# Windowed attention cut into 32-query by 64-key blocks ahead of a tuned Mish feed-forward

## The chip, the cores and the metric

The kernel runs on one core of one Trainium2 chip. The metric is the device time of one execution in microseconds (us). Three executions of the kernel before took 891.72, 894.63 and 894.75 us; the median is 894.63 us.

## The reference, cut to what matters

```python
# q, k, v: (8 batches, 8 heads, 576 positions, 64 per head)
scores = q @ k.transpose(0, 1, 3, 2) / np.sqrt(64)
rel = pos[:, None] - pos[None, :]
mask_plain = (rel >= 0) & (rel < 32)                        # heads 0 to 3
mask_dil = (rel >= 0) & (rel < 128) & (rel % 4 == 0)        # heads 4 to 7
scores = np.where(mask, scores, -1e9)
attn = np.exp(scores - scores.max(-1)); attn /= attn.sum(-1) + 1e-9
x = (attn @ v) laid out as (4608 tokens, 512)
h = x @ w_in                                                # w_in: 512 x 2048
g = h * np.tanh(softplus(h))
out = g @ w_out                                             # w_out: 2048 x 512
```

A query of a plain head sees itself and the 31 keys behind it. A query of a dilated head sees 32 keys too, every fourth one. If the positions are sorted by their residue modulo 4, the dilated heads have the same narrow band within each residue. The weights arrive as 8-byte numbers.

## The kernel before, in words

The 4608 tokens are worked off as 16 units of 288 tokens, two (half 0 and half 1) for each batch. For each unit the attention of eight heads (four pairs of heads: two plain, two dilated) gives x in a transposed layout, split in two float16 parts (hi and lo). The feed-forward then runs on TensorE (PE): `ff1` (L938) multiplies x by w_in, 192 matmuls of 128x128 weights and 288 columns for a unit, ScalarE (ACT) applies Mish, `gate` or `gate_of` splits the result in two float16 parts, and the second product follows. For units 0 to 7 that is `ff2` (L1126): 192 matmuls of 288 columns. For units 8 to 15 (the constant `SEVENS`) it is `product` (L1077): seven half-size products in place of eight, 336 matmuls of 144 columns, with sums of g made by `gate_sums` (L1057) on VectorE (DVE) and sums of w_out made once by `w_sums` (L991, L995) after `rescale` (L976).

The attention works on blocks of 96 queries by 128 keys (plain) and 72 queries by up to 104 keys (dilated, one block for each residue), one pair of heads at a time:

- `scores_of_pair` (L687): the two heads of a pair lie in the upper and the lower 64 partitions, so each matmul uses 64 rows of the array. In units 0 to 2 ("direct") q and k are float32. In the other 13 units ("converted") `prep` scales q and k and splits them in float16 parts (ACT L571, L600, L603, L609; DVE L612, L615; the scale comes by `tops_of`, PE L361 and L368), and each block takes three float16 matmuls.
- `scores` (DVE L711, L717, L719), `exps` (ACT), `transpose_p` (PE L807 for direct units; ACT L795, DVE L797 and a DMA for the others).
- `values` (L830 direct, L836 converted): probabilities times v, 65 columns (64 and the sum), one block and head after another on the full array. For converted units that is three float16 matmuls for each.
- `transpose_x` (DVE L851 writes its input; L869, L891 to L895), which fills x.

The weights (16 halves) are loaded, joined from two words and split by `w_load`, `w_max`, `w_scale`, `w_words` (POOL L446, DVE L448 and L450) and `w_split` (ACT L457, DVE L459) in the first part of the run. `keep_warm` (L1157) issues matmuls of zeros while PE would have nothing else.

The order of all work is a written table, `ORDER`: each word is one step of one function ("ff0.6" is the next step of `ff1(0, 6)`), and each engine executes its instructions in the order in which the table issues them.

Of the kernel before, what the change touches and what calls it, by code (L numbers as in the profile page):

```python
# [10 lines left out]
F16 = mybir.dt.float16  # L11
# [26 lines left out]
MASKED = -2.0 ** 30  # L38
# [3 lines left out]
ld0 mf cs0 cs1 xa1 xa0 kw32 kw22 sp0.1=0 cs3 lv0 lv1 sc0.1 lv0 sp0.0=1 lv1 wl0.3.1 ex0.1 sc0.0 ex0.1 sp0.2=2 ww0.3.1  # L42
sc0.2 wl0.3.0 pr1 ex0.0 pr0 ex0.2 wl0.0.0 ld1 pr0 sp0.3=3 tp0.1=0 ww0.3.0 sc0.3 ex0.2 pr0=2 pr0 ex0.0 tp0.1 tp0.2=1
ex0.3 tp0.2 pr1 pr1 pr0 wl0.0.1 wm0.3.1 va0.2=0 pr0 ex0.3 va0.2 va0.1=1 tp0.3=2 wm0.3.0 va0.2 kw8 tx0.2=3 tp0.0=0
va0.1 va0.1 tx0.1=1 ww0.3.0 wl0.1.1 tp0.3 va0.3=2 ww0.3.1 tx0.2 tx0.2 tp0.0 va0.0=0 tx0.1 ww0.3.0 va0.3 tx0.1 va0.3
kw15 sp1.0=2 wm0.3.0 ww0.3.0 ww0.3.0 va0.0 va0.0 kw5 sp1.2=0 tx0.2 sp1.1=3 wm0.0.0 tx0.1 ww0.0.1 ws0.3=1 ww0.0.0 ld2
sc1.0 ex1.0 tp1.0=2 wm0.0.1 ww0.3.0 sc1.2 tx0.3=0 ex1.2 sc1.1 kw20 pr1=3 tp1.0 kw3 tx0.0=2 tx0.3 tx0.0 ws0.3 ex1.1
sp1.3=1 lv2 tx0.0 tx0.0 pr1 sc1.3 tp1.2=3 ww0.3.1 tp1.2 kw23 va1.2=2 ex1.3 va1.0=3 ww0.0.0 kw15 tp1.3=1 va1.2 va1.0
wp0.3.0 ww0.0.1 tp1.3 va1.2 tx0.3 tx0.3 kw8 ws0.0=2 kw3 tx1.2=1 kw4 tp1.1=0 wp0.3.1 ww0.0.1 ws0.0 wl0.1.0 va1.0
wp0.3.1 tx1.2 kw24 tx1.2 ww0.0.0 tx1.0=2 wp0.3.0 tp1.1 wl0.2.0 va1.3=3 wm0.1.0 va1.1=0 tx1.0 va1.3 va1.1 tx1.0 va1.3  # L50
ww0.1.0 wl0.2.1 wm0.1.1 kw29 ff0.6=3 tx1.0 va1.1 tx1.2 tx1.1=0 tx1.3=2 ww0.1.0 ww0.1.1 ww0.1.1 wp0.0.1 wp0.0.1 ww0.2.0
ff0.6 tx1.3 tx1.1 tx1.1 tx1.3 ws0.1=1 ws0.1 wl1.3.1 wp0.0.0 tx1.3 kw4 ff1.7=0 ff1.7 wm0.2.0 wp0.0.0 ww0.2.1 ww0.2.0
wm0.2.1 ww0.2.1 ff0.1=1 ws0.2=2 ws0.2 ff0.1 wl1.3.0 ft lv2 fs0.0 ff1.1=2 ff1.1 ww0.2.0 fs1 ff1.7 ff1.0=0 pr2 fs0.1
ff1.0 wp0.2.0 ww0.1.1 wp0.2.0 ww0.2.1 fs0.2 ff1.1 ww1.3.1 ff1.6=2 fs0.3 wl1.2.0 wp0.1.1 ff1.0 ff0.6 ww1.2.0 gt1.0=0
ff0.1 fs0.4 wp0.1.1 pr2 ww0.1.0 ff1.6 sp2.3=0 wp0.1.0 ff0.7=3 ww1.3.0 ff0.7 sc2.3 ff0.0=1 wp0.2.1 wp0.1.0 ff1.6 ff0.0
wp0.2.1 wl1.2.1 wm1.3.0 gt1.0 ww1.3.0 ff0.7 wm1.3.1 ww1.3.1 ff1.5=2 ff1.4=3 gt1.3=1 ex2.3 wm1.2.0 ff1.4 gt1.3 ws1.3=0
ff1.5 ff0.0 ww1.3.0 ff1.2=1 ff1.2 gt0.0=2 wm1.2.1 ws1.3 ff1.4 ff1.5 wp1.3.0 gt0.3=3 ww1.2.1 tp2.3=0 ww1.2.0 ww1.3.1
ww1.2.0 wp1.3.0 wp1.3.1 ff1.3=3 tp2.3 ff1.3 ww1.2.1 wl1.0.0 sp2.0=2 pr2 ff1.3 wp1.3.1 ws1.2=0 ff0.5=3 ff0.5 sc2.0
ff1.2 lv3 ww1.2.1 ws1.2 wm1.0.0 ww1.0.0 cs2 ex2.0 wl1.0.1 ff0.2=1 gt0.0 wp1.2.1 gt0.3 ff0.3=0 tp2.0=2 ff0.2 ff0.3
wp1.2.0 ww1.0.1 ww1.0.0 ff0.5 sp2.2=3 tp2.0 pr2=2 ff0.2 wm1.0.1 wp1.2.0 wl1.1.1 wp1.2.1 ff0.4=1 ff0.3 pr2 wl1.1.0 xa3  # L60
va2.0=2 ww1.1.1 gt1.1=4 va2.3=0 va2.0 ww1.0.1 va2.3 gt0.1=5 ww1.0.1 ff0.4 va2.0 sc2.2 va2.3 sp2.1=2 wm1.1.1 wm1.1.0
ff0.4 gt0.2=6 fo0.2.0=1 gt0.1 fo0.3.0 ws1.0=0 gt0.2 ww1.1.0 ex2.2 sc2.1 ws1.0 fo0.3.1 ld3 ex2.1 fo0.3.2 wp1.0.1
# [36 lines left out]
va7.1 pr8 tp7.0=1 ff6.0 fo5.1.3 tp7.0 ff6.1=1 ld9 ff6.1 fo5.3.2 fo5.0.3 sp8.0=2 tx7.1=0 sc8.0 ff6.0 tp7.0=1 ff6.4=0
# [95 lines left out]
QB = 96  # L195
# [1021 lines left out]
```

## Time and profile before

| | before |
|---|---|
| median of three runs | 894.63 us |
| profiled execution, span from first to last instruction | 892.4 us |
| PE busy | 873.6 us (98%) |
| PE weight loads busy | 737.9 us (83%) |
| DVE busy | 705.7 us (79%) |
| ACT busy | 621.1 us (70%) |
| POOL busy | 74.2 us (8%) |

The profile's times are those of one execution, which is given by its span alone; the median stands 2.2 us above that span. Busy PE counts a matmul from its start to its modelled end, so a column of means is longer than the distance between two matmuls that follow each other; the chain of waits gives the distance. PE stands in nearly all of the chain, so the places to look at are the distances on PE, and the early stretch, where the chain's end alone does not say what set the pace.

### The profile page before, as it was taken

The numbers are of one execution on the slowest core, as the hardware profiler recorded it, in microseconds if no ns is written. First come the engines' busy times: TensorE is split into PE (matmuls) and PEld (weight loads), VectorE is DVE, ScalarE is ACT, GpSimd is POOL, SyncE is SP. The second block draws the span as 40 slices with busy tenths as digits, with TensorE's granted clock in tenths as the row PEclk, the third lists the DMA queues.
The fourth block names the chain that finished last, engine by engine and source line by source line (L and its number), as shares of the span: only waits on it lengthen the run. The fifth ranks groups of instructions, "written<-read, shape, count | busy, mean of one in ns | idle before, by whom it ended". The sixth has DMA issues, their size and how long they took to land. (4 is left out here: it accounts for less than half of the span.)

```text
span 892.4 us, 23856 instructions
## 1 busy us (share of the span) xinstructions
PE 873.6 (98%) x10335; PEld 737.9 (83%) x10338; DVE 705.7 (79%) x1035; ACT 621.1 (70%) x924; POOL 74.2 (8%) x123
## 2 busy tenths in 40 slices
PE   9898989999999999999999999999999999999997
PEld 8776768888788878888888788998899898988897
DVE  4888976778879678878899889997999888855453
ACT  5867765874676667797876876858877886844342
POOL 3237463000000000000000000000000000000000
PEclk9999999999999999999999999999999999999999
DMA  9652540326432635253632325235523522122001
GB/s 312 238 189 95 146 143 10 105 72 137 104 68 52 128 74 140 50 130 60 157 85 52 87 43 148 60 86 116 102 67 70 126 58 58 32 59 64 2 15 41
DMA packets 154049, 84.36 MB, mean 95 GB/s; under 512 B 117496, under 2 KB 149848, under 8 KB 153944
## 3 DMA queue, kind: packets, MB, share of 16 engines
q1 hardware_dynamic: 153944, 82.83, 37.5%
q8 instruction: 81, 1.33, 0.6%
q14 instruction: 24, 0.20, 0.1%
HBM read 49.02 MB, written 9.44 MB: 66 GB/s over the span
## 5 line engine op out<-in xcount | busy, mean ns | idle before, releaser
L938 PE MATMUL b<-x,w 128*128 128x288 f16 x3072 | 392.1, 287 | 0.0
L938 PEld LDWEIGHTS <-w 128*128 128x128 f16 x3072 | 298.0, 98 | 75.1 <-issue 0.2
L1126 PE MATMUL b<-g,w 128*128 128x288 f16 x1536 | 198.9, 287 | 0.0
L1126 PEld LDWEIGHTS <-w 128*128 128x128 f16 x1536 | 148.5, 98 | 37.7 <-issue 0.2
L944 ACT ACTIVATE hm<-b,fs 128x576 f32<-128x576 f32 x128 | 92.5, 738 | 78.1 <-PE b L938 63.3
L1077 PE MATMUL b<-g,w 128*128 128x144 f16 x1536 | 101.8, 226 | 0.4 <-DVE y L1096 0.3
L1077 PEld LDWEIGHTS <-w 128*128 128x128 f16 x1536 | 97.6, 98 | 1.6 <-issue 0.6
L1051 DVE SCALAR_TENSOR_TENSOR g<-hm,sg,g 128x1152 f16<-128x1152 f32 (+1 forms) x64 | 79.5, 1261 | 23.3 <-ACT g L1049 23.2
L1049 ACT ACTIVATE g<-hm,sg 128x1152 f16<-128x1152 f32 (+1 forms) x64 | 71.4, 1129 | 15.2 <-PE b L1077 12.0
L758 ACT ACTIVATE sb<-sb,ln_p 72x832 f32<-72x832 f32 (+3 forms) x52 | 46.1, 893 | 18.5 <-DVE sb L719 18.3
L1028 DVE SCALAR_TENSOR_TENSOR g<-hm,sg,g 128x1152 f16<-128x1152 f32 x32 | 46.5, 1462 | 7.1 <-ACT g L1026 7.1
L797 DVE TENSOR_TENSOR p<-sb,p 96x768 f16<-96x768 f32 (+3 forms) x52 | 46.7, 903 | 5.9 <-ACT p L795 5.8
L719 DVE TENSOR_TENSOR sb<-sb,nm 96x512 f32<-96x512 f32 (+4 forms) x64 | 49.2, 768 | 2.2
L717 DVE TENSOR_REDUCE nm<-sb 96x4 f32<-96x512 f32 (+4 forms) x64 | 48.8, 763 | 1.8
L1091 ACT ACTIVATE y<-b,fo 128x288 f32<-128x288 f32 x32 | 25.1, 783 | 35.8 <-PE b L1077 35.7
L1057 DVE TENSOR_TENSOR hm<-hm 128x576 f32<-128x576 f32 x64 | 47.5, 753 | 0.8
L869 DVE TENSOR_TENSOR x<-xs,x 96x384 f16<-96x384 f32 (+1 forms) x52 | 32.0, 615 | 15.9 <-ACT x L867 15.8
L851 DVE TENSOR_TENSOR xs<-b,rec 72x512 f32<-72x512 f32 (+1 forms) x64 | 39.7, 621 | 5.8
L867 ACT CAST x<-xs 96x384 f16<-96x384 f32 (+1 forms) x52 | 29.0, 558 | 21.7 <-DMA x<-x 9.4
L621 POOL MEMSET vh<- 128x12 f16 x26 | 4.2, 167 | 452.9 <-ACT vh L571 390.8
L1077 PE MATMUL b<-g,g 128*128 128x144 f16 x576 | 40.3, 226 | 1.1 <-ACT y L1091 1.1
L795 ACT CAST p<-sb 72x832 f16<-72x832 f32 (+3 forms) x52 | 40.8, 791 | 0.5 <-DMA pT<-p 0.2
(177 smaller groups left out, 1198.1 us busy)
## 6 DMA issues: line engine op xcount, KB each, us to landing
qn<-in_qT SPq DMA_DIRECT2D x16, 576.0 KB
raw<-in_w_out SPq DMA_DIRECT2D x16, 512.0 KB
raw<-in_w_in SPq DMA_DIRECT2D x12, 512.0 KB
out_T<-y SPq DMA_DIRECT2D x32, 144.0 KB
out_T<-y SPq DMA_DIRECT2D x16, 288.0 KB
knd<-in_kdT SPq DMA_DIRECT2D x16, 208.0 KB
vdn<-in_vd SPq DMA_DIRECT2D x7, 416.0 KB
vn<-in_v SPq DMA_DIRECT2D x7, 384.0 KB
```

Of the source, the lines that this page charges most:

```text
L717: nc.vector.tensor_reduce(nm[:nq, :, j:j + n], x, axis=AX.X, op=ALU.max, negate=True)
L719: nc.vector.tensor_tensor(blocked(sb, c0, n, w), x, nm[:nq, :, j:j + n].unsqueeze(3).broadcast_to([nq, 2, n, w]), op=ALU.add)
L758: nc.scalar.activation(x, x, AF.Exp, bias=ln_p[:nq])
L797: nc.vector.tensor_tensor(lo, src, hi, op=ALU.subtract)
L938: nc.tensor.matmul(ph[:, h, :HT], w1[j][:, c, wi, k * P:(k + 1) * P], x_of(d, xi, c), start=(n == 0), stop=(n == len(seq) - 1))
L944: nc.scalar.activation(d["m"][p][:, half, k0:k0 + 2], ph[:, :, :HT], AF.Mish, scale=d["fs"][:, j:j + 1])
L1028: nc.vector.scalar_tensor_tensor(g[:, 1], m, sg, g[:, 0], ALU.mult, ALU.subtract)
L1049: nc.scalar.activation(hi, src, AF.Identity, scale=sg)
L1051: nc.vector.scalar_tensor_tensor(lo, src, sg, hi, ALU.mult, ALU.subtract)
L1057: nc.vector.tensor_tensor(a, a, b, op=op)
L1077: nc.tensor.matmul(acc[e], left(l, e, p, wi)[:, k * P:(k + 1) * P], right(gi, k), start=(n in opens and p == 0 and q == 0), stop=(last and ...
L1126: nc.tensor.matmul(po[:, :HT], w2[:, e, j, wi, k * P:(k + 1) * P], d["g"][j][:, gi, k, :], start=(j == 0 and n == 0), stop=(j == NCH - 1 a ...
```

## The change

It does five things.

1. The attention of a unit is cut anew. A block is 32 queries by 64 keys; three blocks stand side by side as 96 queries. Plain and dilated heads become two *kinds*, and one step handles all four heads of a kind instead of one pair. A matmul of the scores (L573) has 64 rows, 32 columns of weights and 64 streamed columns (56 for the dilated kind of half-0 units from unit 3); the head picks the row half and the block picks one of three 32-column strips of the array. `values` (L673) does the same: 64 keys as rows, 32 queries as weights, 65 streamed columns, so a block's six matmuls lie on six different tiles of the array.
2. Scores are float32 in all units. The scaling and splitting of q and k, and `tops_of`, are gone; the scale of v alone comes by a bf16 matmul (L325). `spread_q` copies the plain q by residue on POOL (L476).
3. v is loaded as 64-key windows, 16 (half 0) or 21 (half 1) of them, that overlap: 12 or 16 DMAs for a unit in runs of 256 bytes. The split of v works on 2048 or 2688 elements of a partition.
4. `SEVENS` begins at unit 3 instead of 8, so `rescale` and all of `w_sums` now come ahead of unit 3's products.
5. `ORDER` is a new table. Biased exponentials, subtraction on PE and the float16 subtraction on PE (L739, L752, L891) are gone.

```diff
-    SEVENS = range(8,16)
+    SEVENS = range(3, 16)

+    def spread_q(u):
+        qp = d["qp"] = pool.tile([P, 2 * HT], F32, name="qp")
+        nc.gpsimd.tensor_copy(qp.rearrange("p (b r i) -> p b r i", r=NR, i=SQ // NR),
+                              d["q"][:, :2 * HT].rearrange("p (b i r) -> p b r i", r=NR, i=SQ // NR))

     def loads_v(u):
+        for h in range(2):
+            for a in range(2):
...
+                nc.sync.dma_start(o[:, :n0], bass.AP(row.tensor, row.offset, [[w, WK], [SQ * w, n0], [1, D]]))
+                for s in range(ns):
...
+                    nc.sync.dma_start(o[:, n0:].rearrange("k (r s) d -> k r s d", s=ns)[:, :, s],
+                                      bass.AP(row.tensor, row.offset, [[w, WK], [2 * RB * w, NR], [1, D]]))

     def prep(u):
-        mr = yield from tops_of(m, 6)
...
+        o = yield from over_partitions(m, 2)
...
-        for x, hi, lo in qparts:
-            nc.vector.tensor_tensor(lo, x, hi, op=ALU.subtract)
...
-        for c, x in zip(ksl, kn):
-            nc.vector.scalar_tensor_tensor(kl[:, c], x, s[:, 1:2], kh[:, c], ALU.mult, ALU.subtract)

-    def scores_of_pair(u, pair):
...
-                for i, (qi, ki) in enumerate([(1, 0), (0, 0), (0, 1)]):
-                    products.append((o, d["q2"][hs, qi, pair, q0:q0 + nq], d["k2"][hs, ki, k0:k0 + nk], i == 0, i == 2))
+    def scores_of_kind(u, kind):
...
+        for a in range(2):
+            for t in range(nb):
+                for s in range(NS):
...
+                    for h in range(2):
+                        hs = slice(h * D, (h + 1) * D)
+                        c = (a * nb + t) * WK
+                        q = d["q"] if kind else d["qp"]
+                        nc.tensor.matmul(pt[s * SQ:(s + 1) * SQ, h, c:c + w], q[hs, q0:q0 + SQ], d["k"][kind][hs, k0:k0 + w],
+                                         start=not d["direct"], stop=True, skip_group_check=True)

     def scores(u, kind):
+            nc.vector.scalar_tensor_tensor(o, i, 1.0 / math.sqrt(D), m, ALU.mult, ALU.add)
+        nc.vector.tensor_reduce(nm[:, :, :n], src, axis=AX.X, op=ALU.max, negate=True)
+        nc.vector.tensor_tensor(dst, src, nm[:, :, :n].unsqueeze(3).broadcast_to([QB, 2, n, w]), op=ALU.add)

     def values(u, pair):
-                for i, (p, vi) in enumerate([(0, 1), (0, 0), (1, 0)]):
-                    c = ((p * 2 + h) * nb + g) * rows
-                    nc.tensor.matmul(avv[:, h, j], pp[:nk, c:c + P], vv[vi][:nk, j, hh, :], start=(i == 0), stop=(i == 2))
+        passes = [(None, 0)] if d["direct"] else [(0, 1), (0, 0), (1, 0)]
+        for t in range(nb):
+            for i, (pi, vi) in enumerate(passes):
+                for s in range(NS):
+                    for h in range(2):
...
+                        nc.tensor.matmul(avv[s * SQ:(s + 1) * SQ, h, t], p[:hk.stop - hk.start],
+                                         vv[vi][hk, window(d, kind, t, s), a, :],
+                                         start=(i == 0), stop=(i == len(passes) - 1), skip_group_check=True)

 ORDER = """
-ld0 mf cs0 cs1 xa1 xa0 kw32 kw22 sp0.1=0 cs3 lv0 lv1 sc0.1 lv0 sp0.0=1 lv1 wl0.3.1 ex0.1 sc0.0 ex0.1 sp0.2=2 ww0.3.1
+wl0.0.1 wm0.0.1 mf ld0 ww0.0.1 qp0 ld0 mf cs1 kw43 sp0.0=0 cs0 wl0.0.0 ld0 ld0 ww0.0.0 ww0.0.1 wm0.0.0 ww0.0.1 ld1
...
```

How the order moves is seen at three places. On the queue of the loads (SP) at the start of the program, the kernel before asks for q, k and v of the first two units (qn, knp, knd; w2 is v's home here) and then for weights:

```order
L487 DMA qn_113<-in_qT 128x1152
L489 DMA knp_115<-in_kT 128x2x288
L492 DMA knd_117<-in_kdT 128x4x72 x2
L513 DMA w2_92<-in_v 128x256
L513 DMA w2_92<-in_v 128x2x256
L514 DMA w2_92<-in_vd 72x4x256
L513 DMA w2_92<-in_v 128x3x256
L514 DMA w2_92<-in_vd 104x4x256
L383 DMA raw_229<-in_w_in 128x512 x2
```

The changed kernel, from the same place, alternates weights with q and k of two units:

```order
L343 DMA raw_111<-in_w_in 128x512 x2
L461 DMA qn_140<-in_qT 128x1152
L466 DMA knp_146<-in_kT 128x2x288
L343 DMA raw_267<-in_w_in 128x512 x2
L470 DMA knd_141<-in_kdT 128x4x80 x2
L461 DMA qk_276<-in_qT 128x1152
L466 DMA knp_285<-in_kT 128x2x320
L343 DMA raw_346<-in_w_in 128x512 x2
L470 DMA qk_276<-in_kdT 128x4x112 x2
L494 DMA w2_90<-in_v 64x8x64
L497 DMA w2_90<-in_vd 64x4x64 x2
```

The first half of w_in moved from behind v to the head of the queue, and v of the first unit moved behind three halves of the weights.

On DVE, also at the start, the kernel before begins with maxima of scores (nm from the banks b); the first instruction on a weight is L448, twenty rows on:

```order
L717 TENSOR_REDUCE nm_214<-b0_70 96x2x2
L717 TENSOR_REDUCE nm_214<-b0_70 96x2
L717 TENSOR_REDUCE nm_236<-b1_71 96x2x2
L717 TENSOR_REDUCE nm_236<-b1_71 96x2
L717 TENSOR_REDUCE nm_252<-b2_72 72x8
```

In the changed kernel the weights' L408 and L410 (L448 and L450 before) stand first, and the subtraction of the maxima (L599) is DVE's in the first units too:

```order
L408 SCALAR_TENSOR_TENSOR w10_86<-w10_86,raw_111 128x1024
L410 SCALAR_TENSOR_TENSOR raw_111<-raw_111,w10_86 128x1024
L598 TENSOR_REDUCE nm_281<-b0_70 96x2x6
L599 TENSOR_TENSOR sb_280<-b0_70,nm_281 96x2x6x64
L408 SCALAR_TENSOR_TENSOR w10_86<-w10_86,raw_267 128x1024
```

The work on the weights moved ahead of the first scores.

On PE, in the middle of a late unit, a dilated pair's scores of the kernel before (24 matmuls, each with its load of weights q2) follow the small matmul of `tops_of` and stand among half-size products:

```order
L1077 MATMUL b2_72<-g1_100,w2_92 128x144
L368 MATMUL b1_71<-cd_10660,ones_74 128x6
L687 LDWEIGHTS q2_10037
L687 MATMUL b3_73<-k2_10087,q2_10037 72x72
L687 LDWEIGHTS q2_10037
L687 MATMUL b3_73<-k2_10087,q2_10037 72x72
```

In the changed kernel the 48 float32 scores of a kind are one row (each brings its own weights):

```order
L773 LDWEIGHTS w10_86
L773 MATMUL b0_70<-x_8583,w10_86 128x288
L573 MATMUL b2_72<-knd_9115,qn_9114 32x56 x48
L912 LDWEIGHTS w2_90
L912 MATMUL b3_73<-g1_98,w2_90 128x144
```

A little ahead of it the values of one dilated pair begin (72 such pairs of rows follow one another there):

```order
L773 LDWEIGHTS w10_86
L773 MATMUL b1_71<-x_8583,w10_86 128x288
L673 LDWEIGHTS pT1_2309
L673 MATMUL b0_70<-vh_8839,pT1_2309 32x65
L673 LDWEIGHTS pT1_2309
```

The four stretches of scores of a unit became two, and the matmul of `tops_of` is gone. Of a whole program, PE's rows hold 1,344 float32 score matmuls (two passes each in the trace) and 3,276 float16 value matmuls now, where there were 1,092 float16 score and 1,092 value matmuls for the converted units.

## Rows read from the trace of the kernel before

**Rows 1.** The page: span, engines, chain by engine and by line.
```profile
span 892.4 us, 23856 instructions
PE 873.6 (98%) x10335; PEld 737.9 (83%) x10338; DVE 705.7 (79%) x1035; ACT 621.1 (70%) x924; POOL 74.2 (8%) x123
PE 43%; ACT 0%; DVE 0%; issue 0%; DVEq 0%
```
**Rows 2.** The chain in order of time, late units: start us, us, what.
```profile
514.13 1.47 PE b L1126 x12
515.91 0.60 PE b L687 x18
...
652.70 1.61 PE b L1077 x24
...
688.14 1.47 PE b L938 x12
...
696.10 1.50 PE b L1077 x24
...
718.94 0.11 PE b L361
...
720.55 0.73 PE b L836 x24
...
724.29 0.31 PE b L368 x2
724.60 0.54 PE b L687 x24
```
**Rows 3.** PE's timeline: start us, us, line, operation, shapes, count.
```profile
16.29 1.25 PE L830 MATMUL b<-vdn,pp 72*72 72x65 f32 x16
17.38 1.18 PE L830 MATMUL b<-vn,pp 128*96 128x65 f32 x12
...
48.40 1.63 PE L938 MATMUL b<-x,w 128*128 128x288 f16 x12
...
70.90 0.74 PE L687 MATMUL b<-knd,qn 64*72 64x72 f32 x16
71.58 10.46 PE L938 MATMUL b<-x,w 128*128 128x288 f16 x84
```
**Rows 4.** Five stretches of 24 us: PE, PEld, DVE, ACT, POOL busy; clock, DMA.
```profile
0.00:24.00 24.00, 22.93 (x263) 19.29 (x263) 12.18 (x30) 13.96 (x28) 8.67 (x23) 1.00 0.97 315
...
72.00:96.00 24.00, 20.37 (x157) 15.47 (x156) 20.05 (x20) 16.62 (x23) 17.95 (x7) 0.86 0.13 45
...
sum 120.00, PE 107.40 PEld 85.77 DVE 95.38 ACT 83.56 POOL 53.91; mean PE 21.48 PEld 17.15 DVE 19.07 ACT 16.71 POOL 10.78
```
**Rows 5.** Two DVE lines of the weights: durations ns min/median/max, first to last start us.
```profile
L448 DVE SCALAR_TENSOR_TENSOR w<-w,raw x15: 678/1217/2120, 20.1 to 129.6; 128x1024 int32<-128x1024 int32 x13, 128x512 int32<-128x512 int32 x2
...
L459 DVE SCALAR_TENSOR_TENSOR w<-raw,ws,w x14: 1267/1274/2151, 42.6 to 141.9; 128x1024 f16<-128x1024 f32 x14
```
**Rows 6.** PE's groups from the start to 141 us: busy us, mean ns.
```profile
L938 PE MATMUL b<-x,w 128*128 128x288 f16 x384 | 51.1, 294 | 0.0
L1126 PE MATMUL b<-g,w 128*128 128x288 f16 x126 | 17.3, 297 | 0.0
```
**Rows 7.** DVE's groups over the run: busy us, mean ns, idle ahead.
```profile
L719 DVE TENSOR_TENSOR sb<-sb,nm 96x768 f32<-96x768 f32 x14 | 13.3, 953 | 0.5
L330 DVE TENSOR_REDUCE m<-vdn 104x1 f32<-104x1024 f32 x7 | 8.4, 1206 | 0.0
...
L895 DVE TENSOR_TENSOR x<-b,x 128x288 f16<-128x288 f32 x3 | 1.7, 564 | 0.0
...
L995 DVE TENSOR_TENSOR g<-g,w 128x1024 f32<-128x1024 f32 x14 | 17.1, 1220 | 0.3
L1028 DVE SCALAR_TENSOR_TENSOR g<-hm,sg,g 128x1152 f16<-128x1152 f32 x32 | 46.5, 1462 | 7.1 <-ACT g L1026 7.1
L1051 DVE SCALAR_TENSOR_TENSOR g<-hm,sg,g 128x1152 f16<-128x1152 f32 (+1 forms) x64 | 79.5, 1261 | 23.3 <-ACT g L1049 23.2
L1057 DVE TENSOR_TENSOR hm<-hm 128x576 f32<-128x576 f32 x64 | 47.5, 753 | 0.8
```
**Rows 8.** PE's loads of weights in the values, over the run.
```profile
L836 PEld LDWEIGHTS <-pT 128*128 128x128 f16 (+2 forms) x1092 | 39.4, 98 | 1.7
```

More of the change, by code (lines that the diff above doesn't have):

```diff
@@ L46 @@
[L46 to L50, printed above, removed]
@@ L191 @@
+fq15.5.1
+""".split()
+ON_DVE = set()
 IN_W2 = 1
@@ L298, in masks_late @@
     def masks_late():
[L299 to L308 removed]
+        pm = take("b", banks)[:QB, 0, :NPB * WK]
@@ L313, in attn_mish_ffn_kernel @@
+        nc.tensor.matmul(pm, ident_p, m_b[:, :NPB * WK], start=True, stop=True)
+        yield
+        m_p.extend(late.tile([QB, 2 * NPB * WK], BF16, name=f"m_p{i}") for i in range(2))
+        nc.scalar.copy(m_p[0].rearrange("p (a k) -> p a k", a=2), pm.unsqueeze(1).broadcast_to([QB, 2, NPB * WK]))
+        nc.scalar.copy(m_p[1].rearrange("p (a k) -> p a k", k=WK),
+                       pm[:, WK:2 * WK].unsqueeze(1).broadcast_to([QB, 2 * NPB, WK]))
     w1 = [const.tile([P, NCC, 2, CH], F16, name=f"w1{g}") for g in range(NCH)]
@@ L507, in loads_v @@
-        d["vn"], d["vdn"] = vn, vdn
-        queue = nc.sync
-        for j0, n in ((0, NPB),) if half else ((0, 1), (1, NPB - 1)):
-            r0 = max(half * HT + j0 * QB - (P - QB), 0)
-            rows = v[b, r0:r0 + P]
-            src = bass.AP(rows.tensor, rows.offset, [list(rows.ap[0]), [QB * rows.ap[0][0], n], list(rows.ap[1])])
-            queue.dma_start(vn[:, j0:j0 + n].rearrange("k j h d -> k j (h d)"), src)
-        queue.dma_start(vdn[:kd].rearrange("k r h d -> k r (h d)"), vd[b, :, i0:i0 + kd, :].rearrange("r k c -> k r c"))
+            vn = w2[:, :2].rearrange("p e j i n -> p (e j i n)").bitcast(F32)[:, :NW * 2 * D]
+        else:
+            vn = late.tile([P, NW * 2 * D], F32, name="vn")
@@ new lines, in prep, with width_of @@
+        d["vh"] = [vh[:, i] for i in range(2)]
+        for i, one in ((0, 1.0), (1, 0.0)):
+            nc.gpsimd.memset(vh[:, i, :, :, D:], one)
+        hi, lo = (x[:, :, :, :D].rearrange("p w a d -> p (w a) d") for x in d["vh"])
+        src = src.rearrange("p w a d -> p (w a) d")
+        nc.scalar.activation(hi, src, AF.Identity, scale=s)
+        yield
+        nc.vector.scalar_tensor_tensor(lo, src, s, hi, ALU.mult, ALU.subtract)
+    def width_of(d, kind):
+        return WD if kind and not d["half"] and not d["direct"] else WK
@@ L809, in transpose_p @@
-        pp = d["p", pair] = early.tile([P, 2, HT], F32, name="pp", bufs=2)
-        yield
-        if pair < 2 and d["half"] == 0:
-            runs = [(QB, 0, QB), (P, QB, HT)]
-        else:
-            runs = [(w, 0, HT)]
-        for n, a, z in runs:
-            nc.scalar.copy(pp[:n, :, a:z], pt[:n, :, a:z])
+        for a in range(2):
+            for t in range(nb):
+                g = a * nb + t
+                nc.tensor.transpose(pt[:, a, t * QB:(t + 1) * QB], sb[:, g * P:(g + 1) * P], ident[:QB, :QB])
```

816 lines of the change are left out of this document (319 added, 497 removed).

## The prediction

> **What bounds the kernel now.** I read the page's busy shares first, then the chain, then the chain in order of time, and last the early stretches. PE is busy for 873.6 of 892.4 us, and the chain, as far back as the profile follows it, is PE with next to nothing else: 43% of the span [rows 1]. So from some point on the time is a sum of distances on PE. In the chain those are: 12 matmuls of 288 columns take 1.47 us (L938 and L1126 alike), 0.1225 us each; 24 half-size ones take 1.50 us, 0.0625 us each; 24 value matmuls take 0.73 us, 0.0304 each; the score stretches take 0.60 us (18 of 128 columns) and 0.54 us (24 of 72 columns) [rows 2]. The feed-forward is then 4608 x 0.1225 + 2688 x 0.0625 = 732.5 us.
>
> The first part is another matter. DVE is busy 12.2 of the first 24 us and 83.2 of the next 96, 87% [rows 4]; the weights are split there, the first word at 20.1 us and the last half at 141.9 us [rows 5]. PE looks full there too, but part of that is filler: at 141 us it had done 384 + 126 matmuls of the feed-forward, 62.5 us of work [rows 6]. I take DVE as what sets the pace until the last half is split at 143.2 us (141.9 + 1.3), and PE after that.
>
> The trace's execution has a span of 892.4 us; the median run is 2.2 us longer. I sum spans and add 2.2.
>
> **Part 1, up to the last split of weights.** In the changed order DVE's list up to its last weight split has the same work on the weights, and beside it: nine more hi/lo subtractions of x at 0.564 us, 5.1 us; four more subtractions of maxima, at 0.95 us for 768 columns and 1.21 for 1024, 4.5 us; the three passes over a dilated kind's scores of unit 3, 3.6 us; one more normalization and maximum of v, about 2 us [rows 7]. Together 15 us more. Against that, its first instruction on weights now waits for the first load of the queue; before it came at 20.1 us, and DVE lay idle for 11.8 of the first 24 us [rows 4, 5]. I give back 8 of these, not all, since v now lands behind three halves of weights and the values wait for it. DVE had 95.4 us done at 120 and at 87% some 115 at 143 [rows 4]. So the last split comes at 24 + (115 + 15 - 20)/0.87 = 150 us, 7 us later. Bounds: nothing given back and the same pace, +17; all given back and 93%, -3. PE's own work of units 0 to 2 gets less (no subtraction on PE, fewer score passes), but I count nothing for it, because DVE covers it; if DVE did not, those are some microseconds of gain. POOL has 17.95 of 24 us at its fullest [rows 4] and gets copies of q and v; I count that at nothing, covered by its idle time elsewhere, with up to 5 us in the upper bound above if weights wait for it.
>
> **Part 2, feed-forward after that.** Five units go from 192 x 0.1225 = 23.5 us to 336 x 0.0625 = 21.0 us [rows 2]: -12.6 us in all, 719.9 us instead of 732.5. By the order, 564 matmuls (69.1 us) stand ahead of the last split, where 62.5 us did. What is left is 650.8 us instead of 670.0: -19.2 us.
>
> DVE pays for it: a unit's gates cost 8 x 1.261 + 8 x 0.753 = 16.1 us instead of 4 x 1.462 = 5.8, and the sums of weights (20 x 1.22 and more) now stand ahead of unit 3's products [rows 7]. Up to the last gate of unit 4 I add up 277 us of DVE work; at 87% that is 24 + 257/0.87 = 319 us. PE needs 150 us plus 177 us of feed-forward plus some 20 us of attention, 347, to get there. So it is covered, with 28 us to spare; if DVE fell below 80% there, PE would wait.
>
> **Part 3, attention of the 13 converted units on PE.** Before, a unit costs: four score stretches, 2.2 us (they cost 0.54 to 0.60, less where two adjoin); 84 value matmuls at 0.0304, 2.55; the two matmuls of the scales, 0.31 + 0.11; the first feed-forward group after scores, 1.61 instead of 1.50, twice, 0.2 [rows 2]. Sum 5.4.
>
> After, the trace has no column strips, only row halves. What it shows of these: 24 matmuls of 72 columns take 0.54 us [rows 2]. At the full 2.4 GHz level 72 columns are 30 ns, so one after another they would be 0.72 us. The two halves run at once: 12 x 30 = 0.36, and 0.18 goes for entering and leaving the mode (18 of 128 columns: 0.48, and 0.12). A float32 matmul is two passes; on the full array 16 passes of 65 columns take 17.38 - 16.29 = 1.09 us, 68 ns, two clocks a column or somewhat more, and 16 passes of 72 columns on row halves take 0.68 us [rows 3], so the halves run at once in float32 too. If all six tiles run at once, a group of scores is 2 x 53 ns and 14 groups are 1.5 us; 42 groups of values at the row's 30.4 ns are 1.28 us: 2.8 us. If the three strips take turns it is three times that, 8.4 us. If in addition the halves did, 17 us, but the rows exclude that. I take 1.2 times the lower end, 3.35 us, because strips are other columns of one array as halves are other rows of it, and the row nearest to them shows no turn-taking. With 75 tile stretches for 13 units in the order, 5.8 each at 0.15 us, 0.87, and the matmul for v's scale, a unit costs 4.3: -1.1 us, -14 us for 13. Bounds: 2.8 + 0.6 (-26 us) to 8.4 + 1.0 (+52 us).
>
> On six tiles the Trainium skill ("TensorE: Matmul & The Clock Gate", Part 3, measured speedup) has a figure: nine tiles in a 3 x 3 packing gave 6.32 times one, at 512 columns. By that, six tiles would run at 0.70 of the ideal, a group would cost 1.42 times the row, and an estimate of the unit is 2.8 x 1.42 + 0.9 = 4.9 us and of the time 876. No row here shows a strip.
>
> Sum: 892.4 + 7 - 19.2 - 14 = 866.2, and with 2.2 the time is 868.
>
> **Hidden edits.** Other engines lose work (half the elements of scores, no splitting of q and k); ACT at 70% and DVE at 79% [rows 1] are not in the chain, so nothing is gained. v's 12 to 16 loads of a unit in place of three stand on SP's queue with the transposes behind them; at some 50 us a unit I count nothing, 5 us if transposes come late.
>
> **Rivals.**
> B, slower: the strips of a row half take turns. For it: nothing in the trace has strips. Against it: halves do not take turns. Place: L573 and L673 in every unit. Price: 8.4 + 0.9 - 5.4 = +3.9 a unit, +51; 892.4 + 7 - 19.2 + 51 + 2.2 = 933. It decides from where a group costs 1.9 times the row: 2.8 x 1.9 + 0.9 = 5.4 + (19.2 - 7)/13.
> B2: a load of weights for a strip waits until matmuls of the same row half are through. Then each of three strips costs a load (36 ns in the values [rows 8]) and a stream in turn: 42 x 3 x 66 ns = 8.3 us of values and 28 x 3 x 89 = 7.5 of scores, with 0.9 some 16.7 a unit, +147; the time is about 1030. Against it: in the values a load of 36 ns and a matmul come every 30.4 ns [rows 2, 8], so loads lie under matmuls of the same rows. The Trainium skill (same page, Part 3, what overlaps) says that loads overlap matmuls only when the row group differs; by that B2 would hold, but this trace disagrees on the full array.
> C, no change: the first part loses. v behind weights, and DVE at 80%, puts the last split at 24 + 118/0.80 = 171 us, 28 us late; with attention at -1.1 or 0 the time is 889 or 903; I price it 893. For it: DVE's waits at the start are for scores and loads; against it: weights, what it works on most, come earlier.
> D, faster: six tiles at full rate (-26) and a start that is not late (-3): 846.
>
> **How the numbers follow.** Forecast 0.54 (own range 850 to 887), B 0.14, B2 0.02, C 0.16, D 0.14. The range 842 to 915 leaves out most of B, B2 and a little of D. Half a per cent is 4.5 us, about what a measurement of this kernel can tell from no change. Faster (below 890): 0.54 + 0.14 + 0.06 of C, 0.74; same 0.08; slower B, B2 and the rest, 0.18.
>
> **What would show it.** Right: stretches of 54 and 72 value matmuls of 0.4 to 0.6 us, 48 scores in 0.8 to 1.1 us, the last weight split near 150 us, PE without gaps after it, half-size matmuls still 62.5 ns apart. Wrong: 72 values in over 1 us (B); last split after 165 us (C); DVE or DMA named in waits of PE between units 3 and 6, which would make the middle of the run, not its ends, what I missed.

## The result, and the profile after

The changed kernel takes 904.77 us (median; 902.42 to 909.76) where the kernel before took 894.69 us beside it: a ratio of 1.0132, 95% interval 1.0098 to 1.0166. It is slower by 1.3%; the forecast was 868 us, faster by 3%. The profiled execution has a span of 900.5 us. All times below are medians of the fast runs: one of e5's ten runs (916 us) and two of e8's ten (4767 us) are left out as slow.

The page of the changed kernel (span, busy shares, chain by engine):

```profile
span 900.5 us, 32620 instructions
PE 848.4 (94%) x14897; PEld 724.8 (80%) x14897; DVE 638.4 (71%) x871; ACT 472.4 (52%) x641; POOL 101.6 (11%) x102
PE 20%; DMA 1%; DVE 1%; issue 0%; SPq 0%; ACT 0%; DVEq 0%
```

Against [rows 1] PE has 25 us less to do, and the span is 8 us longer. The chain now goes back only to 695 us, and it goes through DMAs. The next rows, one long stretch from 150 us to the end, first of before and then of after (length, then PE, PEld, DVE, ACT, POOL busy, clock, DMA share, GB/s), show that all of it is lost there:

```profile
150.00:892.40 742.40, 736.17 (x8954) 627.56 (x8951) 586.60 (x856) 522.53 (x750) 6.90 (x68) 1.00 0.35 80
```
```profile
150.00:900.50 750.50, 722.86 (x12822) 626.54 (x12819) 519.42 (x696) 396.62 (x535) 31.10 (x40) 0.99 0.36 79
```

PE stands idle for 27.6 us instead of 6.2 (in both, some 4.5 of it behind its last matmul). What PE waited for in these stretches, before and after (us in total, times, longest):

```profile
PE b L1077 <- ACT y L1091: 1.1, 2, 0.9
PE b L1077 <- DVE y L1096: 0.3, 1, 0.3
```
```profile
PE b L673 <- DMA pT<-p: 5.4, 2, 4.5
PE b L912 <- DVE y L931: 5.2, 8, 1.0
PE b L573 <- DMA knd<-in_kdT: 2.8, 1, 2.8
PE b L961 <- ACT den L683: 2.7, 1, 2.7
PE b L673 <- issue: 1.8, 2, 1.6
PE b L573 <- issue: 1.5, 2, 1.2
```

Two of the names are DMAs: `pT` are the transposed probabilities that `values` reads, `knd` the keys of the dilated heads. (`den` is the sum by which the probabilities are divided, made by ACT; `y` collects a product's results, by DVE and ACT. "Issue" is idle time for which the profile shows nothing waited for.) The longest wait, 4.5 us, read in the timelines of DVE, SP's queue and PE of the changed kernel (start us, us, engine, line, operation, count):

```profile
503.74 0.95 DVE L637 TENSOR_TENSOR p<-sb,p 96x768 f16<-96x768 f32 x1
```
```profile
505.57 0.60 SPq L494 DMA_DIRECT2D vn<-in_v  x1
506.22 1.96 SPq L497 DMA_DIRECT2D vn<-in_vd  x3
508.29 0.97 SPq L461 DMA_DIRECT2D qn<-in_qT  x1
509.31 0.60 SPq L494 DMA_DIRECT2D vn<-in_v  x1
509.95 1.96 SPq L497 DMA_DIRECT2D vn<-in_vd  x3
511.96 0.61 SPq L494 DMA_DIRECT2D vn<-in_v  x1
512.61 1.97 SPq L497 DMA_DIRECT2D vn<-in_vd  x3
514.68 2.93 SPq L640 DMA_TRANSPOSE pT<-p  x2
```
```profile
518.10 0.69 PE L673 MATMUL b<-vh,pT 64*32 64x65 f16 x54 [4.46 <-DMA pT<-p]
```

The probabilities are ready at 504.7 us. Their transposes go out at 514.7, because 12 of the next unit's 16 loads of v, 0.6 to 0.65 us each, and one load of q stand ahead of them on SP's queue. The second DMA is the same thing with a buffer in it. The chain in order of time:

```profile
700.58 2.37 DVE vh L546
...
702.96 0.62 SPq L494
...
706.09 5.33 DMA knd<-in_kdT
...
711.46 1.10 PE b L573 x48
```

v has one buffer, so its loads wait for DVE's last read at 702.95 us; the keys, which wait for nothing, stand behind them. In both places the granted clock fell to its lower level, 1.2 GHz, before the stall was over, and stayed there for 6.8 us (same columns as the stretches above):

```profile
516.00:522.80 6.80, 4.70 (x89) 4.63 (x90) 1.08 (x2) 0.83 (x2) 0.12 (x1) 0.50 1.19 165
...
710.60:717.40 6.80, 5.94 (x149) 5.08 (x150) 4.59 (x6) 1.43 (x3) 0.47 (x2) 0.50 0.52 106
```

For the sum I counted, from 150 us on, the time from each matmul's start to the next one's; gaps over 0.25 us apart, half of each half-speed stretch apart:

| us | before | after | after without v's loads (e1) |
|---|---|---|---|
| feed-forward (L938, L1126, L1077; L773, L961, L912) | 666.9 | 659.1 | 658.9 |
| attention | 69.5 | 58.5 | 58.4 |
| gaps | 1.1 | 22.9 | 12.3 |
| lost to the lower clock | 0 | 5.4 | 0 |

The work fell by 18.8 us; gaps and clock took 27.2 back. Without v's loads 16.0 of the 27.2 are gone.

### The profile page after: what moved, and what is told of

Same layout as the page of the kernel before. It is cut to its first block, busy times and chain, and to the rows that moved or that the text cites. A ratio compares the mean times of both kernels' runs of the same rounds, so it can differ in the third digit from the quotient of the medians.

```text
span 900.5 us, 32620 instructions
## 1 busy us (share of the span) xinstructions
PE 848.4 (94%) x14897; PEld 724.8 (80%) x14897; DVE 638.4 (71%) x871; ACT 472.4 (52%) x641; POOL 101.6 (11%) x102
## 2 busy tenths in 40 slices
DMA packets 194986, 86.33 MB, mean 96 GB/s; under 512 B 170272, under 2 KB 190752, under 8 KB 194848
## 5 line engine op out<-in xcount | busy, mean ns | idle before, releaser
L773 PE MATMUL b<-x,w 128*128 128x288 f16 x3072 | 400.2, 287 | 1.9 <-ACT den L683 0.5
L773 PEld LDWEIGHTS <-w 128*128 128x128 f16 x3072 | 294.4, 98 | 78.3 <-issue 3.2
L912 PE MATMUL b<-g,w 128*128 128x144 f16 x2496 | 166.6, 226 | 6.1 <-DVE y L931 4.5
L912 PEld LDWEIGHTS <-w 128*128 128x128 f16 x2496 | 158.4, 98 | 10.0 <-issue 6.3
L886 DVE SCALAR_TENSOR_TENSOR g<-hm,sg,g 128x1152 f16<-128x1152 f32 (+1 forms) x104 | 130.9, 1270 | 31.5 <-PE b L773 16.5
L884 ACT ACTIVATE g<-hm,sg 128x1152 f16<-128x1152 f32 (+1 forms) x104 | 116.2, 1128 | 45.8 <-PE b L912 30.6
L931 DVE SCALAR_TENSOR_TENSOR y<-b,fo,y 128x144 f32<-128x144 f32 x78 | 33.5, 476 | 73.1 <-PE b L912 48.9
L476 POOL COPY qp<-qn 128x576 f32<-128x576 f32 x15 | 27.9, 1862 | 461.1 <-DMA qn<-in_qT 352.6
L961 PE MATMUL b<-g,w 128*128 128x288 f16 x576 | 73.6, 286 | 2.7 <-ACT den L683 2.7
L961 PEld LDWEIGHTS <-w 128*128 128x128 f16 x576 | 55.6, 98 | 17.1 <-issue 2.9
L912 PE MATMUL b<-g,late_sums 128*128 128x144 f16 x936 | 68.4, 231 | 0.7 <-DVE y L931 0.7
L912 PE MATMUL b<-g,g 128*128 128x144 f16 x936 | 67.2, 227 | 1.3 <-issue 0.8
L912 PEld LDWEIGHTS <-late_sums 128*128 128x128 f16 x936 | 62.9, 100 | 1.9 <-DVE y L931 1.1
L912 PEld LDWEIGHTS <-g 128*128 128x128 f16 x936 | 61.0, 98 | 3.4 <-issue 1.7
L689 DVE TENSOR_TENSOR xs<-b,rec 96x384 f32<-96x384 f32 (+1 forms) x64 | 39.7, 621 | 6.9 <-PE b L725 1.1
L673 PEld LDWEIGHTS <-pT 64*32 64x32 f16 (+1 forms) x3276 | 30.0, 91 | 16.5 <-issue 8.1
```

The costliest lines, as they stand in the source:

```text
L673: nc.tensor.matmul(avv[s * SQ:(s + 1) * SQ, h, t], p[:hk.stop - hk.start], vv[vi][hk, window(d, kind, t, s), a, :], start=(i == 0), stop=( ...
L689: nc.vector.tensor_tensor(xs[:, :nb].rearrange("p j (h e) -> p h j e", h=2), avv[:, :, :, :D], rc.unsqueeze(3).broadcast_to([QB, 2, nb, D] ...
L773: nc.tensor.matmul(ph[:, h, :HT], w1[j][:, c, wi, k * P:(k + 1) * P], x_of(d, xi, c), start=(n == 0), stop=(n == len(seq) - 1))
L884: nc.scalar.activation(hi, src, AF.Identity, scale=sg)
L886: nc.vector.scalar_tensor_tensor(lo, src, sg, hi, ALU.mult, ALU.subtract)
L912: nc.tensor.matmul(acc[e], left(l, e, p, wi)[:, k * P:(k + 1) * P], right(gi, k), start=(n in opens and p == 0 and q == 0), stop=(last and ...
```

## The experiments

Four theories. 1: v's loads on SP's queue are the loss. 2: the loss is spread, and the stalls only took slack. 3: the clock at the start. 4: DVE is filled up ahead of unit 3. Beside each run the kernel before took 894.45 to 895.02 us, so the runs can be compared with each other and with the 904.8 us of the changed kernel.

**e1, no loads of v from unit 4 on.**
```diff
...
+        if u > DIRECT:
+            d["vn"] = U[DIRECT]["vn"][:, :sum(nw)]
+            return
```


> From unit 4 on no value rows are loaded; every unit works on those of unit 3. It leaves out 12 to 16 DMA issues a unit on SP's queue and their traffic. Theory 1: each of these issues holds SP's queue for about 0.62 us, so 10 us a unit, and the transposes and keys behind them land late. The changed kernel's PE waited 0.91 + 4.46 us for pT and 2.84 us for knd after 150 us, and TensorE's granted clock fell to half after the last two, which cost some 3.4 us each: 15 us in all, so 904.8 - 15 = 890 us (885 to 894), and no wait of PE for a DMA is left after 150 us. Theory 2 (the lost time is spread over the waits for y, the gaps named issue and DVE's queue; the two stalls only took the slack of others): at most a third of it, 900 us or more.


Measured 885.5 us, 0.987 of before (0.9817 to 0.9924): 19.3 us less than with them, more than the 15 expected. PE's waits after 150 us:
```profile
PE b L916 <- DVE y L935: 4.8, 8, 1.0
PE b L577 <- issue: 2.1, 2, 1.2
PE b L677 <- issue: 1.9, 2, 1.5
PE b L965 <- ACT den L687: 1.4, 1, 1.4
...
PE b L677 <- DMA pT<-p: 0.4, 1, 0.4
```
The long DMA waits are gone, and the wait for `den` is halved. In the changed kernel ACT, which makes `den`, had stood 4.30 us in front of it for a transposition of x from the same queue (3.11 us in e1):
```profile
192.40 0.51 ACT L715 CAST x<-xs 96x384 f16<-96x384 f32 x1 [4.30 <-DMA x<-x]
```
Theory 2 falls as the main cause; the gaps that are left (12.3 us) are not those loads'. The edit takes away the issues, the bytes and the wait for the buffer together; the next runs keep the bytes and the buffer, and change the engine, the place and the number.

**e2, v's loads by POOL, and by ACT.**
```diff
-                nc.sync.dma_start(
+                (nc.sync if d["direct"] else nc.gpsimd).dma_start(      # e2_v_by_act: nc.scalar
...
```


> All loads of the value rows from unit 3 on are issued by POOL, which is busy for 11% of the span, instead of SP; bytes and packets stay. Theory 1 with the queue as its cause: the waits for pT and knd go as they do without the loads, 890 us, up to 896 if POOL's copies of q (1.9 us each) come late behind loads that wait for their buffer. Theory 1 with the traffic as its cause (the loads' packets slow the transposes down): the stalls stay and it ends at 900 to 905 us. Theory 2: 900 us or more as well, but with the waits for pT and knd gone.

> The same loads issued by ACT. ACT is busy for 52% of the span, and in the changed kernel the loads waited 36.5 us in nine places for DVE's last use of the buffer; on ACT these waits stand ahead of the gates, the exponentials and Mish. If the place of a wait in an in-order queue is what costs, this is no better than SP: 900 to 920 us, with PE waiting for what ACT writes (hm, g, y). If only SP's 0.62 us an issue counted, it would come to 890 to 895 us, as with POOL.


POOL 934.98 us (1.0389 to 1.0495 of before), ACT 929.31 (1.031 to 1.0419): both far worse than SP. ACT came out on the side that I expected, and beyond its 920 us. POOL did not: its own queue waited, for the buffer and for something that the profile calls issue, and v was late. Nor did the packets stay, as I had written: the program's fell from 194,986 to 137,002, so this run changes more than the queue.
```profile
POOL vn L494 <- DVE vh L546: 156.8, 7, 36.3
POOL vn L497 <- issue: 109.5, 67, 4.5
POOL vn L494 <- issue: 96.8, 28, 54.5
```
The Trainium skill ("DMA: Bandwidth & Descriptors", Issuing engines are not separate DMA queues) says that issuing from several engines saves only sequencer time, "usually small relative to the DMA itself". The runs agree that another engine doesn't help; that the time is small they don't bear out, 0.62 us an issue against 2.6 to 2.8 us to land.

**e5, fillers in the two stalls.** In `ORDER`, `kw` is `keep_warm`, `sp` scores, `va` values, `lv` the loads of v, `tp` the transposes of probabilities, `ld` the loads of q and k, `fq` a half-size product.
```diff
-va10.0=3        sp15.1=3
+kw100 va10.0=3  kw60 sp15.1=3
```


> 100 filler products ahead of the values of unit 10 and 60 ahead of the last dilated scores, in the two places where PE stood idle for 4.46 and 2.84 us; the queues are as they were. If the two stretches of about 6.8 us at half the clock come from these stalls, the clock is held at 1.00 there and 2 x 3.4 = 6.8 us come back: 898 us. If the clock's fall has another cause, it stays, and so does 905 us. The waits themselves stay in both.


906.04 us, with runs from 899 to 911. In the profiled one (910.92) the second fall of the clock is gone, a shorter one is left at 529 us (3.4 us instead of 6.8), and others came at 198 and 317 us behind stalls of 5.7 and 2.8 us. So stalls do not stand at fixed places with fixed sizes, and the price of the clock by itself stays unmeasured.

**e6, half as many loads; e8, later loads; e7, both.**
```diff
-                nc.sync.dma_start(o[:, :n0], bass.AP(row.tensor, row.offset, [[w, WK], [SQ * w, n0], [1, D]]))
+            nc.sync.dma_start(o[:, :n0].rearrange("k w a d -> k w (a d)"),        # both heads of a half, rows side by side
+                              bass.AP(row.tensor, row.offset, [[w, WK], [SQ * w, n0], [1, w]]))
...
-lv11 ... lv11 lv11 lv11 tp10.0 tp10.1 ... lv15 ld15
+tp10.0 tp10.1 lv11 ... lv11 ... lv11 ... lv11 ... ld15 lv15
```


> The value rows are laid out in memory so that the two heads of a partition half stand side by side, and a unit's 12 to 16 loads become 6 to 8 of twice the size; the same bytes go into the same buffer, in the same order among the other transfers. Leaving all of them out gave 885.5 us against 904.8 us, 19 us. Theory 1 with the queue's 0.62 us an issue as the cause: about half of the 10 us a unit is gone, so half or more of the 19 us: 893 us (888 to 897). If a wait for the buffer ahead of the loads is the cause, and not their number, the transposes stand behind it as before: 900 us or more.

> Only the order of SP's queue is changed, at two places: the four steps of loads of unit 11 come after the transposes of unit 10 (and the first maximum of unit 11 right ahead of its second), the first step of loads of unit 15 after its keys. Number, size and bytes of the transfers stay. Theory 1 with the place in the queue as its cause: the stalls of 4.46 and 2.84 us and the two half-speed stretches go, 14 us: 891 us (888 to 896). If the loads' number or traffic costs wherever they stand, the waits only move: 899 us or more.

> Both: half as many loads of value rows, and those of units 11 and 15 moved behind the transposes of unit 10 and the keys of unit 15. By Theory 1 nearly all of the 19 us that the loads cost: 888 us (884 to 893), no wait of PE for pT or knd over 1 us, and the granted clock at 1.00 from 80 us on. By Theory 2 no better than 900 us.


896.24, 897.1 and 894.71 us (ratios to before 1.0004 to 1.0035, 0.998 to 1.005, 0.9977 to 1.0017). Each of the first two gives back some 8 of the 19 us; together they give 10. In e8 the stalls at 513 and 708 us are gone with the same number and bytes of loads, so the place in the queue is part of the cause. I had expected 891 and 888. In e8's profiled execution (902.33) PE waited 6.5 us for `den` at 204 us, where the order is the changed kernel's; this wait was 2.7 us there, 5.7 in e5 and e13 and 1.4 to 1.9 in e1 and the runs with fewer loads. So other places of the queue cost too, and not the same in each execution. In e6 and e7 the packets became fewer with the loads (155,304 in e6), so these two alone don't tell which of the two helps; e11 does.

**e11, twice as many loads.**
```diff
+                for j0, j1 in [(0, n0)] if d["direct"] else [(0, n0 // 2), (n0 // 2, n0)]:
...
+                    for r, m in [(0, NR)] if d["direct"] else [(0, NR // 2), (NR // 2, NR // 2)]:
```


> The other way: every load of value rows from unit 3 on is cut in two, 24 to 32 issues a unit instead of 12 to 16, with the same bytes in the same places. So far no issue gave 885.5, 6 to 8 gave 896.2, 12 to 16 gave 904.8 us. Theory 1 (an issue's 0.62 us on SP's queue is the price): 10 us more a unit on the queue, and 15 to 25 us on the time: 918 to 930 us, with more waits of PE for pT, knd and what stands behind them. If the bytes, their packets or the wait for the one buffer were the price, the number would not matter: 903 to 908 us.


972.2 us (1.0805 to 1.0884), 67 us more with the same bytes and nearly the same packets (197,931 against 194,986); I had expected 15 to 25. PE's waits after 150 us:
```profile
PE b L677 <- DMA pT<-p: 16.3, 2, 15.3
PE b L916 <- DVE y L935: 11.6, 8, 7.3
PE b L965 <- ACT den L687: 9.7, 1, 9.7
```
None, half, all and twice the issues gave 885.5, 896.2, 904.8 and 972.2 us: 11, 9 and 67 us more. From 150 to 850 us SP spent 23, 31, 40 and 56% of its time on issuing (30% in the kernel before) and another 33, 30, 27 and 20% waiting at the head of its queue for a buffer or a result. The queue wasn't full in any of these runs; what stood behind an issue was late all the same.

**e10, more fillers at the start; e13, no sums of w_out.**
```diff
-kw43 ... kw9 sp0.1 ... kw66
+kw118 ... kw39 sp0.1 ... kw100
```
```diff
-            return sums[n - 1][e][j][i]
+            return w2[:, e, j, i]
...
     def w_sums(e):

+        return
```


> Another matter: 139 more filler products in the first 30 us, in three places where PE waits. The granted clock was 0.79, 0.86 and 0.86 in the first three stretches of 24 us, against 1.00, 0.86 and 0.98 in the kernel before. Theory 3: this clock costs the start up to 11.8 us of PE's time, and holding it gives 5 us or more back: below 900 us. Theory 1 says that the start is bound by what it waits for (the first split of unit 0's products and the weights), as the equal FFN work left at 150 us has it: 903 to 906 us whatever the clock.

> The sums of w_out are left out (the products read w_out itself in their place), so DVE and ACT lose this work, which filled DVE to 49.6 of 50 us between 250 and 300 us, ahead of unit 3's first product. Theory 4 (half-size from unit 3 pays for itself by filling DVE there): the gaps of PE from 235 to 332 us, 4.5 us of which about 2 name DVE or what it writes, go, and time with them: 900 us or below. Theory 1: at most 2 us, 902.5 to 905 us.


906.56 us (898.21 to 907.58) and 906.29 us (903.35 to 908.46). In e10 the clock's mean over the first 72 us was 0.93 instead of 0.83, and the median did not move. (Runs with the changed kernel's own start show 0.81 in e1 to 0.95 in e11, so the fillers need not be the reason; and by 150 us e1, e10 and e11 had made 570, 575 and 576 of the feed-forward's 288-column matmuls, the changed kernel 574, so this clock didn't set the pace.) In e13 DVE had 27 us less to do, and nothing came of it. Theories 3 and 4 fall.

**e9, two products one place earlier.**
```diff
-fq9.6.0 ... fq10.0.0=1     fq11.6.0 ... fq12.0.0=2
+fq10.0.0=1 fq9.6.0 ...     fq12.0.0=2 fq11.6.0 ...
```


> The two edits to the loads together (894.7 us), and the first product of units 10 and 12 ahead of the sixth of the unit before, where PE stood for 0.95 us for y in each case. By the trace 2 x 0.95 = 1.9 us go: 892.8 us (890 to 896), and the waits for y fall from 5.0 to about 3 us. If such a wait only moves to the next product that uses the bank: 894 to 896 us.


893.05 us (0.9952 to 0.9998 of before), and the waits for y fell from 5.0 to 3.0 us. These two microseconds come from the new order; the difference from e7's time, 1.7 us, lies within the spread of either run.

**e14, v in memory window by window; e15, that with e9's order.**
```diff
-                nc.sync.dma_start(o[:, :n0], bass.AP(row.tensor, row.offset, [[w, WK], [SQ * w, n0], [1, D]]))
...
+        src = v[b, half].rearrange("p (w a d) -> p w a d", w=NW, a=2)
+        nc.sync.dma_start(vn[:, :n0], src[:, :n0])
...
+        nc.sync.dma_start(vn[:, n0:], src[:, n0:sum(nw)])
```


> The value rows lie in memory window by window, as the buffer wants them (a row that stands in two windows is stored twice), so that a unit's loads are 2 issues of 128 partitions with long pieces instead of 12 to 16 of 64; the bytes that they bring and the order of the work are the changed kernel's. Theory 1 (the issues on SP's queue): close to the run without these loads, 887 us (884 to 891). If the bytes themselves or the wait for the one buffer cost, it stays at or above the run with half as many issues, 896 us.

> The same layout with the loads of units 11 and 15 behind the transposes and keys, and the first products of units 10 and 12 one place earlier. Theory 1: with 2 issues a unit the places no longer matter, only the two waits for y do: 2 us below the run with the layout alone, 885 us (881 to 889), faster than the kernel before by 1%. If the places still matter, 4 us or more below it.


889.48 us (0.9911 to 0.9955) and 887.56 us (0.9873 to 0.994). Both beat both kernels, e15 the kernel before by 0.9%. The bytes are there, and most of the 19.3 us is back, but not all of it in the same place. After 150 us gaps and lower clock cost 28.3 us in the changed kernel, 12.3 in e1 and 19.4 in e14. The rest of e14's gain lies in the start, where the first units' loads became fewer too: by 150 us e14 had made 621 of the feed-forward's 288-column matmuls and e15 622, the changed kernel 574, 5.8 us of work less, and the last split of weights ended at 145.2 us instead of 151.9. (e16 below, with the same start, had 580; runs with the changed kernel's start had 544 to 577.) The packets fell as well, to 120,231. e15's long stretch after 150 us has 19.8 us of idle PE, where the changed kernel has 27.6:
```profile
150.00:881.80 731.80, 712.00 (x12703) 617.16 (x12700) 516.69 (x692) 395.72 (x534) 29.06 (x37) 1.00 0.32 80
```

**e16, one pass of values in place of three.**
```diff
-        passes = [(None, 0)] if d["direct"] else [(0, 1), (0, 0), (1, 0)]
+        passes = [(None, 0)] if d["direct"] else [(0, 0)]
```


> With that layout, of the three passes of the values of each converted unit only one is made (the products of the low parts are left out), so 2184 of 3276 tile products go and every stretch of them stays. Attention after 150 us took 58 us of PE's time against 64 before, where the forecast had a gain of 14. If a tile product has its own price, 9.9 ns as in the changed kernel's trace, 21.6 us go, and the gain was smaller because the kernel before had less to lose: 865 us. If a stretch has a fixed price (its start, the first loads, the slower products of the FFN behind it), less than 12 us go: 875 us or more.


864.8 us, 24.7 less than e14. (The 64 us named there left out the matmuls of the scales, L361 and L368, 5.4 us: attention went from 69.5 to 58.5.) In the two profiled executions, which are 20.2 us apart, the values fell by the same count from 32.5 to 12.1 us, 9.4 ns for each product that went, so a product has its own price. Gaps and lower clock fell from 19.4 to 13.8 us; it was the gaps that the profile calls issue that went, while waits for y rose from 5.0 to 7.4. The gaps called issue after 150 us, in e14 and in e16:
```profile
PE b L665 <- issue: 4.3, 4, 1.4
PE b L765 <- issue: 2.5, 1, 2.5
PE b L565 <- issue: 1.9, 2, 1.0
PE b L904 <- issue: 0.7, 2, 0.5
```
```profile
PE b L765 <- issue: 0.6, 1, 0.6
```

## Why the prediction was wrong

**The step that failed** is in the hidden edits: "v's 12 to 16 loads of a unit in place of three stand on SP's queue with the transposes behind them; at some 50 us a unit I count nothing, 5 us if transposes come late." It named the place and set the price at zero. The price is 19.3 us by the medians (e1) and 16.5 between the two profiled executions. Of the sum's error, 900.5 - 866.2 = 34.3 us, gaps and clock after 150 us are 27.2, of which e1 takes 16.0 away; the other 7 us are work, by Part 3. I had asked whether 10 us of issues fit into 50 us, a question of share; what counts in an in-order queue is what stands behind the ten. The range ended at 915 and held the result, but by luck: it was that wide for strips that take turns and for a late start, and neither came. The forecast's sign was wrong.

**Part 1** held in its number. The changed kernel's DVE lines of the weights (durations min/median/max, first to last start):
```profile
L408 DVE SCALAR_TENSOR_TENSOR w<-w,raw x15: 678/1224/1697, 7.4 to 136.8; 128x1024 int32<-128x1024 int32 x13, 128x512 int32<-128x512 int32 x2
```
```profile
L419 DVE SCALAR_TENSOR_TENSOR w<-raw,ws,w x14: 1271/1278/2118, 22.1 to 150.6; 128x1024 f16<-128x1024 f32 x14
```
The first word is 13 us earlier and the last half 9 us later than in [rows 5]; the last split ended at 151.9 us, where the forecast had 150. That was partly luck. Up to that time DVE was busy for 120.8 us, only 4.6 more than the 116.2 of before up to its last split, where the sum had 15 more; and in the first 24 us it got 13.3 us done, 1.1 more than before, where the sum gave back 8. The errors largely cancel. "PE without gaps after it" did not hold.

**Part 2** held in its count: at 150 us the matmuls left were 649.6 us of feed-forward (forecast 650.8; before 663.0 at that time). Half-size matmuls are still 62.5 ns apart. The changed kernel's chain, late:
```profile
790.30 3.00 PE b L912 x48
...
805.94 1.50 PE b L912 x24
...
808.91 0.68 PE b L673 x72
809.59 3.11 PE b L912 x48
```

**Part 3** had the right direction and a term too small. 72 values take 0.68 us. The 48 scores of a dilated kind are 96 rows of the trace, two passes each, and took 1.00 to 1.21 us in the eight stretches that were not cut; the 48 rows in 1.10 us shown above are half of them, at the lower clock.
```profile
501.90 1.28 PE L573 MATMUL b<-knd,qn 64*32 64x64 f32 x96
503.11 0.92 PE L912 MATMUL b<-g,g 128*128 128x144 f16 x12
```
So tiles do work at once, and rivals B and B2 are out. But six values cost 59 ns (9.9 each): between the row's 30.4, for tiles that all run at once, and three times that, for strips in turn. The sum had 1.2 times the row, 36.5: 12.5 us too little over 13 units. By e16 the price is one of each product, and not of a group of six. Scores came to 147 ns a group against 127. The rows at 808.91 and 809.59 us show the stretch's other price, 48 products in 3.11 us behind values and 3.00 elsewhere; that was in the forecast as 0.15 us and held: the feed-forward's 659.1 us is 9.5 more than its count (3.9 before), 0.13 for each of 75 stretches. In all, attention gave 5.4 us, not 14. The figure from the Trainium skill ("TensorE: Matmul & The Clock Gate", Part 3, measured speedup) had led to 4.9 us a unit; (58.5 + 9.5)/13 = 5.2 was measured, so it was nearer than my 4.3. One reading of B2's was off: the 36 ns for a load of weights are [rows 8]'s busy time divided by the count; the row's mean of one load is 98 ns.

**Rivals.** None of them was what happened: B and B2 fall by the stretches, C by the last split, and D needed a start that is not late and tiles at full rate, and had neither. Of the signs that I had named for being wrong, DVE or a DMA in PE's waits between units 3 and 6 came, but small: 2.3 us for DVE and 0.9 us for pT, from 264 to 332 us. The long DMA waits came later, in units 10 and 15.

**What stays open.** Why a run without v's loads (e1) still has 11 us more gaps than before is told only in part: some 4 us are more waits for y than before (e9 took 2 by a change of the order), some 4 the gaps called issue. And e14 stays 4 us above e1, although its start is ahead. By the traces that isn't waits for a DMA (1.0 us against 0.4) but the gaps called issue: 9.4 us against 4.0. They are 7.8 to 8.6 us in e6, e7, e9 and e15 too, and 4.1 in the changed kernel; why larger loads come with more of them is open.

## What to carry to other kernels

Price a DMA not by its bytes or its share of time, but by what stands behind it in its in-order queue: list, for each load added, the next transfer that an engine waits for. Lay data out so that a buffer comes in one or two issues; that was worth 15 us here, up to 6 of them at the start, and moving the loads to another engine cost 25 to 30. And don't take such a cost as proportional: the first 10 us of issues a unit cost 19 us of the run, the next 10 cost 67.

## What the runs showed of the hardware

- An issue of a load of v took SP 0.62 us in the median at 64 KB and at 128 to 144 KB alike, 0.61 at 32 KB (e11) and 0.62 at 256 to 288 KB (e6), so the number sets the time. With e14's long pieces it took less: 0.35 us at 512 KB, 0.57 at 576 to 768 KB. But two transposes of probabilities behind such a load took 7.85 us, where two took 2.93 above; another two took 7.23 without one just ahead. Over the run these transposes took 1.90 us each in e14 and 1.69 in the changed kernel. Why was not tested.
- The gaps called issue. The changed kernel fetched 116 packets on the queue that the page names instruction, 16 KB each, before 81 and e16 99. Its two gaps of over 1 us called issue, both in a tile stretch, began 0.7 and 1.2 us after the start of one; in the longest of e14, 2.5 us, one started 0.2 us after the gap's beginning. Their near disappearance in e16 fits a PE that runs out of instructions when products are 10 ns long. This was seen, not tested by itself, and it doesn't explain why e14 has twice as many as the changed kernel.
- On six 64x32 tiles a float16 product of 65 columns came every 9.9 ns, 11.1 ns when a stretch has only 18 or 24 of them, and one of the two passes of a float32 score (56 or 64 columns) every 12.2 ns.
